# Attention and MLP decode step with gradients: query weights in pairs of groups, row vectors in fixed places, wider products, grad_out first, a new order

## The chip, the cores and the metric

The kernel runs on one core of a Trainium2 chip. The metric is device time in microseconds from start to end of one execution; the number compared is the median of several runs of the same kernel. The profile is that of one further execution, taken by the hardware profiler.

The engines named below are PE (matrix products; PEld is its loading of weights), DVE (vector), ACT (scalar), POOL (GpSimd) and SP, which here only issues transfers. Sixteen DMA engines move the data between HBM and the on-chip memory SBUF. Results of PE land in PSUM banks, and DVE or ACT must copy ("evict") them to SBUF before a transfer can store them.

## What is computed

One decode step of a layer, and all gradients of it for a given `grad_out`:

```python
def _A_ref(x, k_cache, v_cache, wq, wo):        # B=2, Sq=1, D=576, Hq=32, Hkv=16, Sk=4096, Dh=128
    q = (x @ wq).reshape(B, Sq, Hq, Dh).transpose(0, 2, 1, 3)
    k, v = jnp.repeat(k_cache, 2, axis=1), jnp.repeat(v_cache, 2, axis=1)
    scores = jnp.einsum("bhqd,bhkd->bhqk", q, k) * (Dh ** -0.5)
    p = softmax(scores)
    o = jnp.einsum("bhqk,bhkd->bhqd", p, v)
    return o.transpose(0, 2, 1, 3).reshape(B, Sq, Hq * Dh) @ wo
def _B_ref(x, w_gate, w_up, w_down):             # F=4608
    return ((x @ w_gate) * (x @ w_up)) @ w_down
xn = layernorm(A_x)
out = A_x + _A_ref(xn, A_k_cache, A_v_cache, A_wq, A_wo) + _B_ref(xn, B_w_gate, B_w_up, B_w_down)
# returned: out and the gradients of A_x, A_k_cache, A_v_cache, A_wq, A_wo, B_w_gate, B_w_up, B_w_down
```

All tensors are bfloat16. With two tokens there is little arithmetic per byte: every cache and weight is read once, and a gradient of the same size is written for each of them. Since there are only two tokens, each gradient is a sum of very few outer products.

## The kernel before

**Groups and steps.** The 16 key/value heads are worked in eight groups of two heads (four query heads each). A group and one of the two batch entries make a step; there are 16 steps. For a step the kernel loads two key tiles and two value tiles of 1 MB (`load_kv`, L1108; 8 KB per partition), transposes each on DVE (`turn`, L1175; the transposing helper is L464), forms scores and their gradients on PE (`score`, L1228, matmuls L1234), the softmax (L1283) and its gradient (L1339), contracts with the caches (`contract`, L1390, matmuls L1407), and writes the gradients of the caches as outer products (`head_outer`, L1244, matmuls L1255) against block-diagonal stationaries that POOL builds (L1222). Each such gradient tile of 1 MB takes four evictions of 128x1024 (L468 on ACT, L470 on DVE) into a staging tile, and then one store (`put`, L687, issued at L691).

**Per group.** `group_front` (L954) forms the query rows from the group's query weights and, from `grad_out`, the gradient of the attention output; `group_back` (L1020) closes a group: it adds to `acc` (L1060) and, with the transposed query weights, to `accx` (L1085), and starts the gradients of `wo` (`rows_outer`, L729) and of `wq`. Between the two calls the group's query weights stay on chip. They come in three transfers (`load_w`, L1123): two tails of 64 rows with 512 bytes each (L1132) and the main part of 512 rows with 1 KB each (L1136). They live in the ring `ww`, together with the weights `wo` and `w_down`.

**The MLP** is worked in nine slices of 512 columns (`mlp`, L838); gate and up weights come for two slices at a time (L1155, L1158), with rows of 2 KB.

**Row vectors.** A weight gradient such as that of `wq` is the outer product of the normalized input `xnr` (32-row quadrants of it) with a row vector, the tile Q for one group or D for one MLP slice. Q and D come from rings of six and five separate tiles. Gradients of several groups or slices are written together (`wide_outer`, L767): four groups, or four slices. For them `wide_unit` (L752) runs a matmul of 128 columns for every group and quadrant into one PSUM bank (L759):

```python
for j, rhs in enumerate(rhss):
    for aa in range(2):
        a = 2 * A + aa
        nc.tensor.matmul(o[:, aa, j * P:(j + 1) * P], lhsT=xnr[32 * a:32 * a + 32, dc * P:(dc + 1) * P],
                         rhs=rhs(a), start=True, stop=True)
```

The last 64 of the 576 rows go separately (`tail_outer`, L808, tiles `tl`, stores of 64 KB).

**Buffers.** One pool of 16 tiles of 8 KB per partition (`big`) serves keys and values as loaded (`kv`, at most 7), transposed tiles (`X`, at most 15), staging tiles (`st`, at most 4) and gate/up weights (`G`, at most 2).

**Order.** The kernel sets the order of all instructions on each engine while it is built. Each piece of work is a generator that yields requests: an operation on an engine with an estimated cost, a buffer (ACQ, REL), a wait for an event, a transfer (DMA). The class `Order` (L105) simulates these with a model of the transfers (`Lines`, constants `LM`, `LAG`) and, whenever an engine is free, takes the request with the lowest priority number among those that can start within a slack. The priorities are `pr(name, s)`: 28 per step, plus tables of offsets by kind and step (`PR`, `HEAD`, `TAIL`, `OFF`) and start points (`MLP_AT`, `WQ_AT`, `WO_AT`). The result is one fixed list per engine. All loads and stores but those of the inputs `A_x` and `grad_out` stand in the one list of SP, so that a store whose data aren't ready holds back the loads behind it. `A_x` and `grad_out` are issued by ACT (L597), and the layer norm waits for both.

Of the kernel before, what the change touches and what calls it, by code (L numbers as in the profile page):

```python
# [13 lines left out]
P = 128  # L14
# [90 lines left out]
class Order:  # L105
# [3 lines left out]
    def __init__(self):  # L109
        self.free = {e: 0.0 for e in ("PE", "ACT", "DVE", "POOL", "SP")}  # L110
        self.slots = {}
        self.home, self.cap, self.used = {}, {}, {}
        self.lines = Lines()
        self.quad, self.kind = (None, 0.0, 0.0), None
        self.streams = []
        self.count = 0
        self.log = []
        self.lanes = {"HW": [], "SW": []}
# [17 lines left out]
    def advance(self, s, value):  # L136
        while True:
# [13 lines left out]
            elif kind == "spawn":  # L151
                self.spawn(s.req[1], s.req[2], s.ready)
            elif kind == "prio":
                s.prio = (s.req[1], s.prio[1])
            elif kind == "lset":
                s.req[1].t = Late(s.land)
            elif kind == "lrel":
                self.pool(s.req[1])[s.req[2]] = s.land
                if s.req[1] in self.used:
                    self.used[s.req[1]] -= 1  # L160
            else:
                return

# [31 lines left out]
    def run(self):  # L195
        while self.streams:
# [8 lines left out]
            if e is not None:  # L205
                t, _, s, e = min((c for c in cand if c[3] == e and c[0] <= t + SLACK[e]), key=lambda c: (c[1], c[0]))
# [27 lines left out]
            elif r[0] == "dma":  # L234
                self.free[e] = t + r[2]
                s.land = self.lines.push(e == "POOL", t + r[2] + LATENCY[e], r[3], r[4])
# [54 lines left out]
def DMA(engine, cost, nbytes, row=8192):  # L291
# [5 lines left out]
NBIG, NGU, NWW, NBD = 16, 1, 6, 3  # L297
CAP = {"kv": 7, "X": 15, "st": 4, "G": 2}
OFF = {"mload": {0: 96.4, 1: -26.1, 2: 880.0, 3: 94.9, 4: -346.4, 5: -156.4, 6: -87.6, 7: 8.9, 8: 146.0, 9: -13.8,
       10: 91.2, 11: -99.0, 12: -61.7, 13: 103.4, 14: 404.9, 15: -150.5}, "wload": {0: -50.8, 1: -238.8, 3: -315.1,  # L300
# [7 lines left out]
       "load": {0: 195.1, 2: 227.9, 3: -17.9, 4: -185.2, 5: -111.1, 6: -195.0, 7: -157.8, 8: 475.0, 10: 90.3,  # L308
       11: -45.9, 12: -113.2, 13: 340.9, 14: 38.7, 15: -10.9}, "front": {1: -351.4, 2: 56.5, 3: 55.5, 4: 1100.6,
       5: 44.1, 6: -364.2, 7: -8.3, 8: -150.0, 10: 278.3, 11: -217.9, 12: 25.9, 14: -46.2, 15: 809.6},  # L310
       "turn0": {0: -96.0, 1: 186.1, 2: 128.2, 3: 344.6, 4: 259.4, 5: 502.5, 6: 22.0, 7: -80.7, 8: 79.6, 9: -81.7,
       10: -397.2, 11: -241.3, 12: -223.5, 13: -195.7, 14: 186.3, 15: 55.8}, "con": {0: -121.6, 1: 346.9, 2: 7.7,
# [3 lines left out]
       "back": {0: 413.0, 1: -6.1, 2: 233.5, 3: 588.7, 4: 263.1, 5: -92.6, 6: -1063.1, 7: 111.3, 8: 44.4, 10: -315.0,  # L316
# [3 lines left out]
       11: -7.4, 12: 14.8, 13: 23.1, 14: 398.8, 15: -591.6}, "dsc": {0: -130.6, 2: -312.2, 3: -339.0, 4: 207.7,  # L320
       5: -530.4, 6: 41.2, 7: 323.6, 8: -0.4, 9: 644.8, 10: -274.2, 11: 125.7, 12: 309.5, 13: -43.5, 14: 192.2,
       15: -0.7}, "mlp": {0: 81.6, 1: -71.7, 2: 147.3, 3: -224.1, 4: -6.3, 5: 14.7, 6: 616.7, 7: -152.4, 8: -159.9,
       9: 42.7, 10: -45.7, 11: 24.0, 12: 245.6, 13: -6.0, 14: -127.2, 15: -22.4}, "att": {0: 251.8, 1: -520.9,
       2: 62.8, 3: 21.5, 4: -199.3, 5: -366.7, 6: 546.7, 7: -109.6, 8: -638.2, 9: 1.5, 10: -174.3, 11: 113.2,
       12: 18.4, 13: -79.6, 14: -31.8, 15: -12.4}, "conv": {1: 208.9, 2: -233.1, 3: 119.4, 4: 0.3, 5: -102.3,
       6: -60.5, 8: 9.6, 9: -114.9, 10: 102.5, 11: 45.1, 12: 165.0, 13: -36.7, 14: 23.6, 15: -54.5}}
MLP_AT = [1.22, 5.43, 16.39, 14.23, 25.87, 33.08, 39.74, 38.29, 101.55]
WQ_AT = [-2, 5, 9, 22, 32, 30, 50, 47]
WO_AT = [-10, -14, -8, 3, 37, 36, 48, 48]
# [6 lines left out]
HEAD = {"turn0": -109.2, "turn1": -1091.6, "att": -224.6, "dsc": -208.3, "con": 390.9, "out1": -1503.4,  # L336
        "out0": 772.1, "front": 803.5, "back": -715.7, "W0": 1770.6, "W1": 26.3, "BD1": 1384.3, "BD0": 3893.2,
        "conv": -396.6, "load": 469.8}
TAIL = {"turn0": -167.6, "turn1": 1451.8, "att": -1608.9, "dsc": 1030.3, "con": 1577.7, "conv": 3.8, "out1": 2595.4,
        "out0": -474.0, "front": -576.5, "back": 355.2, "W1": 698.1, "BD1": -2114.1, "BD0": 951.5, "load": 618.9,  # L340
        "W0": 381.9}
PR = {"turn0": 410.8, "turn1": -89.2, "att": -1586.1, "dsc": -1566.9, "conv": 32.7, "con": -332.6, "out1": 2476.3,
      "out0": 866.1, "front": 94.3, "back": -196.2, "W0": -1406.3, "W1": -128.9, "BD1": 1706.7, "BD0": -477.7,
      "mlp": -490.2, "wout": -771.6, "store": -4.6, "load": 401.7, "wload": -1959.2, "fin": -1327.7, "const": 3504.2,
      "mload": -416.2}
# [8 lines left out]
def kernel(  # L354
# [45 lines left out]
    WB = 4 * FS + 256  # L400
# [10 lines left out]
    kv_t = X_t = st_t = G_t = tiles("big", NBIG, [P, NCH * Dh])  # L411
# [4 lines left out]
    tl_t = tiles("tl", 2, [P, FS])  # L416
    BD_t = tiles("BD", NBD, [P, 16, Dh])
# [3 lines left out]
    D_t = tiles("D", 5, [P, 2, P])  # L421
# [12 lines left out]
    Q_t = tiles("Q", 6, [P, P])  # L434
# [125 lines left out]
    Emore, Ein, Eprep = Event(), Event(), Event()  # L560
# [19 lines left out]
    def front_y():  # L580
        yield WAIT(Ein)
# [11 lines left out]
    def front():  # L593
        xb, yb = xy[:, 0:D], xy[:, D:2 * D]
        for t, src in ((xb, A_x), (yb, grad_out)):
            yield DMA("ACT", 0.45, 2304, 1152)
            nc.scalar.dma_start(t, src.rearrange("b s d -> (b s) d"))  # L597
        yield ("lset", Ein)
        yield SPAWN(front_y(), -999.0)
# [61 lines left out]
    def stationaries(i, rep, npos, half, costs):  # L661
# [6 lines left out]
        for h in range(2):  # L668
# [5 lines left out]
    def dxn(dp, i, X, S, pos, xoff, xstep, Xt, St, toff, tpos):  # L674
# [6 lines left out]
        for s in range(St):  # L681
            for q in range(4):
                nc.tensor.matmul(dp[32 * q:32 * q + 32, P:160], lhsT=view(Wt[:], 0, P, 8 * tpos(q, s), [[1, 32]]),
                                 rhs=view(Xt, 0, P, toff(q, s), [[2, 32]]),
# [67 lines left out]
    def wide_unit(rhss, dc, A, st, off):  # L752
        n = len(rhss)

        def mms(o):
            for j, rhs in enumerate(rhss):
                for aa in range(2):
                    a = 2 * A + aa
                    nc.tensor.matmul(o[:, aa, j * P:(j + 1) * P], lhsT=xnr[32 * a:32 * a + 32, dc * P:(dc + 1) * P],  # L759
                                     rhs=rhs(a), start=True, stop=True)  # L760
# [4 lines left out]
        return mms, (0.053 * n, 0.052 * n), 2 * P * n, ev  # L765

    def wide_outer(rhss, dst, p, event):  # L767
        width, last = FS * len(rhss), []
        for d0 in (0, 2):
            i = yield ACQ("st")  # L770
# [5 lines left out]
            for c in range(2):  # L776
                for A in range(2):
                    yield SPAWN(unit(*wide_unit(rhss, d0 + c, A, st_t[i], c * width), done[2 * c + A]), p)
# [780 lines left out]
```

## Time and profile before

| | us |
|---|---|
| median of 3 runs | 477.73 |
| lowest, highest | 476.86, 479.79 |
| the profiled execution, whole | 480.7 |
| its span, first to last instruction | 478.9 |

| engine | busy us | share of span | instructions |
|---|---|---|---|
| PE | 375.8 | 78% | 6538 |
| PEld | 214.9 | 45% | 6538 |
| DVE | 369.2 | 77% | 708 |
| ACT | 335.6 | 70% | 507 |
| POOL | 152.0 | 32% | 208 |

The granted PE clock is 0.70 on average, changing between half and full speed. In 41,925 packets 185.95 MB are moved, 388 GB/s on average: 92.48 MB read from HBM and 92.48 MB written.

The profile's page shows the span in 40 slices of 12 us; a digit is the busy share in tenths, DMA is the mean over the 16 engines. "SPq L691 <- ACT big L468" means that SP's list stood at a store (L691) until an eviction on ACT (L468) was done; the three numbers are the sum in us, the count and the longest. A transfer line ends with its size in KB and the median time from issue to landing in us. In a group's line stand the output and input tiles, the count, the busy time, the mean duration in ns and the idle time before it.

### The profile page before, as it was taken

The page shows a single profiled execution, that of the slowest core. Times are in us where ns is not written, and L with a number is a line of the kernel's source. Part 1 is how long each engine was busy: PE and PEld are TensorE (multiplying, and loading weights), DVE is VectorE, ACT ScalarE, POOL GpSimd, SP SyncE. Part 2 cuts the span into 40 slices and gives each one's busy share as a digit, 9 for nine tenths or more (in the row PEclk, how much of TensorE's full clock was granted, in tenths as well). Part 3 has the DMA queues.
Part 4 walks back from the last instruction along what each step waited for, and adds up shares of the span by engine and source line. Part 5 has one row for each costly group of instructions (what it writes and reads, how often), then busy time and mean ns, then how long its engine had stood idle before and what let it go on. Part 6 is the DMA issues. An engine that isn't in the chain of part 4 may idle for free.

```text
span 478.9 us, 15380 instructions
## 1 busy us (share of the span) xinstructions
PE 375.8 (78%) x6538; PEld 214.9 (45%) x6538; DVE 369.2 (77%) x708; ACT 335.6 (70%) x507; POOL 152.0 (32%) x208
## 2 busy tenths in 40 slices
PE   1668588989878877768878986599887769898894
PEld 1545353545554534446344453464444424444452
DVE  8788787867867976786956987889677958888781
ACT  3139659966787693833869875399776978897871
POOL 0440074343003643003434530032644556333000
PEclk9979676556766677885567595859656876656876
DMA  8999999999999999999999999999999999999994
GB/s 299 355 405 419 391 402 380 353 377 422 422 400 371 395 365 393 423 414 389 316 399 384 354 402 422 421 413 406 346 414 415 418 419 422 419 417 391 425 369 187
DMA packets 41925, 185.95 MB, mean 388 GB/s; under 512 B 3960, under 2 KB 13440, under 8 KB 25472
## 3 DMA queue, kind: packets, MB, share of 16 engines
q1 hardware_dynamic: 41848, 184.96, 98.3%
q8 instruction: 51, 0.84, 0.7%
q14 instruction: 18, 0.15, 0.1%
q10 hardware_dynamic: 8, 0.00, 0.0%
HBM read 92.48 MB, written 92.48 MB: 386 GB/s over the span
## 4 chain that ended last, share of the span: by engine, by line
DMA 46%; PE 25%; DVE 14%; ACT 8%; issue 3%; SPq 2%; POOL 1%; DVEq 0%; ACTq 0%; POOLq 0%
DMA out_dram<-big 18%; DMA big<-in_A_v_cache_dram 15%; DVE big L464 8%; ACT big L468 7%; PE ps_o L1255 4%; DMA big<-in_A_k_cache_dram 4%; PE ps_m L1234 4%; PE ps_m L1407 4%; PE ps_o L722 3%; DMA gu<-in_B_w_up_dram 3%; DMA ww<-in_A_wo_dram 3%; DMA big<-in_B_w_gate_dram 2%; DVE big L470 2%; PE ps_m L678 1%; PE ps_o L759 1%
## 5 line engine op out<-in xcount | busy, mean ns | idle before, releaser
L468 ACT CAST big<-ps_o 128x1024 bf16<-128x1024 f32 (+2 forms) x310 | 277.6, 958 | 47.6 <-PE ps_o L1255 18.9
L464 DVE STREAM_TRANSPOSE big<-big 128x1024 f32<-128x1024 f32 x146 | 175.9, 1224 | 29.7 <-DMA out_dram<-big 16.2
L1222 POOL TENSOR_TENSOR BD<-vr,mask 128x2048 bf16<-128x2048 bf16 x32 | 115.3, 3603 | 105.4 <-ACT vr L468 49.8
L470 DVE CAST big<-ps_o 128x1024 bf16<-128x1024 f32 (+2 forms) x68 | 74.2, 1093 | 16.4 <-PE ps_o L722 7.4
L1234 PE MATMUL ps_m<-big,W 128*32 128x128 bf16 x2048 | 59.9, 282 | 11.3 <-DVE cr L1359 2.6
L1234 PEld LDWEIGHTS <-W 128*32 128x32 bf16 x2048 | 46.7, 125 | 27.9 <-issue 25.7
L1255 PE MATMUL ps_o<-BD,dd 32*128 32x512 bf16 x256 | 45.8, 480 | 9.9 <-ACT big L468 7.9
L671 POOL COPY wt<-wm 64x128 bf16<-64x128 bf16 (+1 forms) x34 | 8.9, 261 | 138.2 <-DVE wm L664 119.5
L1255 PE MATMUL ps_o<-BD,pp 32*128 32x512 bf16 x256 | 48.2, 520 | 5.5 <-ACT big L468 4.0
L1199 POOL COPY W<-rep 32x16 bf16<-32x16 bf16 x128 | 24.5, 192 | 55.8 <-DVE rep L983 33.6
L464 DVE STREAM_TRANSPOSE big<-ww 128x1152 f32<-128x1152 f32 x25 | 34.0, 1359 | 7.7 <-DMA ww<-in_B_w_down_dram 3.5
L1407 PE MATMUL ps_m<-big,pp 128*32 128x512 bf16 x256 | 30.2, 547 | 3.8 <-DMA big<-in_A_v_cache_dram 3.3
L1255 PEld LDWEIGHTS <-dd 32*128 32x128 bf16 x256 | 12.2, 98 | 32.1 <-issue 27.6
L1407 PE MATMUL ps_m<-big,dd 128*32 128x512 bf16 x256 | 25.8, 491 | 0.4 <-DVE oT L1427 0.2
L1255 PEld LDWEIGHTS <-pp 32*128 32x128 bf16 x256 | 10.4, 97 | 28.1 <-issue 24.2
L872 PE MATMUL ps_m<-big,Wdy 128*128 128x128 bf16 x162 | 15.4, 269 | 4.8 <-DVE rz L1320 3.1
L722 PE MATMUL ps_o<-dyr,hb 32*32 32x288 bf16 x288 | 18.0, 382 | 0.2 <-ACT big L468 0.2
L759 PEld LDWEIGHTS <-xnr 32*128 32x128 bf16 x368 | 12.9, 116 | 10.8 <-issue 9.7
L722 PE MATMUL ps_o<-dyr,R 32*32 32x288 bf16 x256 | 16.2, 378 | 1.3 <-ACT big L468 0.9
L872 PEld LDWEIGHTS <-Wdy 128*128 128x128 bf16 x162 | 13.6, 121 | 6.8 <-issue 6.7
L759 PE MATMUL ps_o<-D,xnr 32*128 32x128 bf16 x256 | 13.0, 276 | 3.9 <-issue 2.2
L1308 ACT COPY mr<-m 1x128 f32<-1x128 f32 x16 | 4.7, 295 | 15.8 <-DVE m L1306 15.6
(205 smaller groups left out, 487.3 us busy)
## 6 DMA issues: line engine op xcount, KB each, us to landing
out_dram<-big SPq DMA_DIRECT2D x74, 1024.0 KB, 12.8
big<-in_A_k_cache_dram SPq DMA_DIRECT2D x32, 1024.0 KB, 12.7
big<-in_A_v_cache_dram SPq DMA_DIRECT2D x32, 1024.0 KB, 13.2
out_dram<-big SPq DMA_DIRECT2D x17, 576.0 KB, 10.7
ww<-in_B_w_down_dram SPq DMA_DIRECT2D x9, 576.0 KB, 13.5
ww<-in_A_wo_dram SPq DMA_DIRECT2D x8, 576.0 KB, 7.3
ww<-in_A_wq_dram SPq DMA_DIRECT2D x8, 512.0 KB, 8.0
big<-in_B_w_gate_dram SPq DMA_DIRECT2D x4, 1024.0 KB, 12.3
```

Of the source, the lines that this page charges most:

```text
L464: nc.vector.transpose(out, in_)
L468: nc.scalar.copy(out, in_)
L470: nc.vector.tensor_copy(out=out, in_=in_)
L671: nc.gpsimd.tensor_copy(view(Wt[:], 64 * h, 64, 0, [[dims[-1][1], n], [1, dims[-1][1]]]), view(Wm[:], 64 * h, 64, off, dims))
L722: nc.tensor.matmul(o[32 * q:32 * q + 32, aa, 0:HD2], lhsT=view(t, 32 * q, 32, 2 * A + aa, [[4, 32]]), rhs=dyr[32 * q:32 * q + 32, k * HD2: ...
L759: nc.tensor.matmul(o[:, aa, j * P:(j + 1) * P], lhsT=xnr[32 * a:32 * a + 32, dc * P:(dc + 1) * P], rhs=rhs(a), start=True, stop=True)
L872: nc.tensor.matmul(dh, lhsT=Wdy[:, e, 2 * k:2 * k + P], rhs=view(X[:], 0, P, 64 * k + e, [[D, FC], [2, 32]]), start=(k == 0 and e == 0), s ...
L1199: nc.gpsimd.tensor_copy(view(W_t[t][w][:], 32 * a, 32, 6 + 8 * a, [[G * WW, 4], [WW, G], [1, 2]]), view(rep_t[grp[g]["qs"]][:], 32 * a, 32 ...
L1222: nc.gpsimd.tensor_tensor(BD_t[i][:], view(vr_t[v][:], 0, P, 0, [[0, 16], [1, Dh]]), view(mask16[:], 0, P, 0, [[1, 16], [0, Dh]]), ALU.mult)
L1234: nc.tensor.matmul(sc[32 * cq:32 * cq + 32, :], lhsT=view(W[:], 0, P, (be * G + l) * WW + 6 - 4 * c2 - 2 * l, [[1, 32]]), rhs=view(X[:], 0 ...
L1255: nc.tensor.matmul(o[:, k, :], lhsT=pr2[32 * c4:32 * c4 + 32, :], rhs=BD[32 * c4:32 * c4 + 32, 8 * l + 4 * h2:8 * l + 4 * h2 + 4, :], star ...
L1407: nc.tensor.matmul(ct[32 * j:32 * j + 32, :], lhsT=view(rT, 0, P, 4 * c + 2 * l, [[1, 32]]), rhs=kv_t[kvS[s][t][l]][:, Dh * c:Dh * (c + 4) ...
```

## The change

- **Query weights.** The first two groups still come alone (1 KB rows), the other six in three pairs: one main transfer of 512 rows with 2 KB each, and two tails of 64 rows with 1 KB. They no longer live in the ring `ww` (6 tiles, now 4) but in the pool `big` (16, now 17), at most two of its tiles, and their tails in a new ring `qt` of two tiles. A pair's tile is released when the second of its groups has transposed its half. `group_front` and `group_back` read their half of the tile; in `group_back` the tail takes 16 narrow matmuls over 64 partitions in place of 8 over 128.
- **Row vectors** Q and D lie side by side in one tile each, with four fixed places (group or slice modulo four).
- **Wider products.** `wide_unit` runs one matmul over up to 512 columns for each quadrant.
- **grad_out** is loaded first on SP, ahead of the first keys; the layer norm waits for `A_x` alone.
- **Staging.** The caps of the pool change (`X` 15 to 8, `st` 4 to 9). The second tile of a head's pair, and the second half of a wide product, ask for their staging tile only after some evictions of the first.
- **Order.** All priorities, start points, slacks and the constants `LM` and `LAG` are new. The planner can now weigh loads against stores on SP (`ALT`), with a weight of 0.

```diff
-NBIG, NGU, NWW, NBD = 16, 1, 6, 3
-CAP = {"kv": 7, "X": 15, "st": 4, "G": 2}
+NBIG, NGU, NWW, NBD = 17, 1, 4, 3
+CAP = {"kv": 7, "X": 8, "st": 9, "G": 2, "wq": 2}
...
-LM, LAG = 0.67, 1.7
+LM, LAG = 0.24, 2.75
...
-BIAS = 0.196
-SLACK = {"PE": 0, "ACT": 0.21, "DVE": 0.48, "POOL": 937075237.61, "SP": 6210463039.22}
+BIAS = 0.091
+SLACK = {"PE": 0.07, "ACT": 0.32, "DVE": 0.47, "POOL": 1756923746230.71, "SP": 2641436507915.03}
...
     def front_y():
-        yield WAIT(Ein)
+        yield DMA("SP", 0.36, 2304, 1152)
+        nc.sync.dma_start(xy[:, D:2 * D], grad_out.rearrange("b s d -> (b s) d"))
+        yield ("lset", Eiy)
+        yield PRIO(-999.0)
+        yield WAIT(Eiy)
...
-    def wide_unit(rhss, dc, A, st, off):
-        n = len(rhss)
-
+    def wide_unit(rhs, n, dc, A, st, off):
         def mms(o):
-            for j, rhs in enumerate(rhss):
-                for aa in range(2):
-                    a = 2 * A + aa
-                    nc.tensor.matmul(o[:, aa, j * P:(j + 1) * P], lhsT=xnr[32 * a:32 * a + 32, dc * P:(dc + 1) * P],
-                                     rhs=rhs(a), start=True, stop=True)
+            for aa in range(2):
+                a = 2 * A + aa
+                nc.tensor.matmul(o[:, aa, 0:n * P], lhsT=xnr[32 * a:32 * a + 32, dc * P:(dc + 1) * P],
+                                 rhs=rhs(a), start=True, stop=True)
...
+    def q_rhs(g, n=1):
+        return lambda a: view(Q_all[:], 32 * a, 32, P * (g % 4), [[P, n], [1, P]])
...
+    def free_wq(pair):
+        yield WAIT(*pair["turned"])
+        yield REL("wq", pair["w"])
+        yield REL("qt", pair["t"])
...
-        yield DVE(1.37)
-        t32(pairs(X[:, 0:WB]), pairs(wq[:]))
-        yield REL("ww", st["wq"])
+        yield DVE(1.25)
+        t32(pairs(X[:, 0:4 * FS]).rearrange("p (c n) -> p c n", c=4),
+            pairs(wq[:]).rearrange("p (c n) -> p c n", c=4)[:, :, HFS * j:HFS * (j + 1)])
+        yield DVE(0.4)
+        t32(pairs(X[64 * j:64 * j + 64, 4 * FS:5 * FS]), pairs(wt[64 * j:64 * j + 64, :]))
+        yield SET(pair["turned"][j])
...
+                js = [j] if i < 2 else [0, 1] if j == 0 else []
+                for k in js:
+                    yield DMA("SP", 0.36, 64 * FS * 2, 1024)
+                    nc.sync.dma_start(t[64 * k:64 * k + 64, :], A_wq[512:576, n0 + FS * (k - j):n0 + FS * (k - j) + FS])
+                if js:
+                    yield ("lset", *[grp[i + k - j]["Lq"] for k in js])
+                    width = FS * len(js)
+                    yield DMA("SP", 0.4, 128 * 4 * width * 2, 2 * width)
+                    nc.sync.dma_start(w[:].rearrange("p (c n) -> p c n", n=2 * FS)[:, :, FS * js[0]:FS * js[0] + width],
+                                      A_wq[0:512, n0:n0 + width].rearrange("(c p) n -> p c n", p=P))
...
-    def head_outer(s, t, l, pr2, done):
+    def head_outer(s, t, l, pr2, done, after):
         g, b = divmod(s, Bq)
+        yield WAIT(*after)
         i = yield ACQ("st")
...
+    od.spawn(front_y(), -2e5)
```

More of the change, by code (lines that the diff above doesn't have):

```diff
@@ L115, in __init__ @@
         self.streams = []
+        self.last = None
         self.count = 0
@@ L155, in advance @@
             elif kind == "lset":
-                s.req[1].t = Late(s.land)
+                for e in s.req[1:]:
+                    e.t = Late(s.land)
             elif kind == "lrel":
@@ L162, in advance, with again, stores @@
                 return
+    def again(self, s, e):
+        return ALT if e == "SP" and self.stores(s) == self.last else 0.0
+    def stores(self, s):
+        return s.gen.__name__ in ("put", "final_out", "final_dx")
     def start(self, s):
@@ L205, in run @@
             if e is not None:
-                t, _, s, e = min((c for c in cand if c[3] == e and c[0] <= t + SLACK[e]), key=lambda c: (c[1], c[0]))
+                t, _, s, e = min((c for c in cand if c[3] == e and c[0] <= t + SLACK[e]),
+                                 key=lambda c: (c[1][0] + self.again(c[2], e), c[1][1], c[0]))
             r = s.req
@@ L235, in run @@
                 self.free[e] = t + r[2]
+                if e == "SP":
+                    self.last = self.stores(s)
                 s.land = self.lines.push(e == "POOL", t + r[2] + LATENCY[e], r[3], r[4])
@@ L339 @@
[L339 to L345, printed above, removed]
+ALT = 0.0
@@ L348, in pr @@
+PR = {"turn0": 544.1, "turn1": -318.2, "att": -1984.1, "dsc": -1493.2, "conv": 288.5, "con": -530.9, "out1": 1889.6,
+      "out0": 1063.4, "front": -189.5, "back": -267.9, "W0": -1094.9, "W1": 243.2, "BD1": 1052.4, "BD0": -299.5,
+      "mlp": -247.6, "wout": -893.4, "store": -2106.8, "load": 1804.4, "wload": -2440.2, "fin": -496.9,
+      "const": 3883.5, "mload": -2076.5}
 def pr(name, s):
@@ L409, in tiles @@
         return [const.tile(list(shape), dtype, name=f"{tag}{i}") for i in range(n)]
-    kv_t = X_t = st_t = G_t = tiles("big", NBIG, [P, NCH * Dh])
+    kv_t = X_t = st_t = G_t = wq_t = tiles("big", NBIG, [P, NCH * Dh])
     od.share("big", CAP)
@@ L416 @@
     tl_t = tiles("tl", 2, [P, FS])
+    qt_t = tiles("qt", 2, [P, FS])
     BD_t = tiles("BD", NBD, [P, 16, Dh])
@@ L433 @@
     R_t = tiles("R", 2, [P, P])
-    Q_t = tiles("Q", 6, [P, P])
+    Q_all = const.tile([P, 4, P], BF16, name="Qall")
+    D_all = const.tile([P, 4, 2, P], BF16, name="Dall")
+    for i in range(4):
+        od.ring(f"Q{i}", 1)
+        od.ring(f"D{i}", 1)
     pp_t = tiles("pp", 2, [P, 2, P])
@@ L593, in front @@
     def front():
[L594 to L597, printed above, removed]
+        xb = xy[:, 0:D]
+        yield DMA("ACT", 0.45, 2304, 1152)
+        nc.scalar.dma_start(xb, A_x.rearrange("b s d -> (b s) d"))
         yield ("lset", Ein)
-        yield SPAWN(front_y(), -999.0)
         yield ACT(1.5)
@@ L667, in stationaries @@
         yield POOL(costs[1])
-        for h in range(2):
+        for h in hs:
             off, dims = half(h)
@@ L1167, in load_w @@
                 yield SPAWN(mlp(k, hh, sl, Lgu, Ld, d), pr("mlp", MLP_AT[k] / 4))
+    wqs = [dict(turned=events(2)) for _ in range(NG // 2)]
     def load_ws(items):
```

154 lines of the change are left out of this document (82 added, 72 removed), and 23 rows, old and new, of the table OFF.

## The prediction

> **What bounds the kernel now.** I read the slices of the page first, then its DMA queues.
>
> ```profile
> DMA  8999999999999999999999999999999999999994
> GB/s 299 355 405 419 391 402 380 353 377 422 422 400 371 395 365 393 423 414 389 316 399 384 354 402 422 421 413 406 346 414 415 418 419 422 419 417 391 425 369 187
> ...
> q1 hardware_dynamic: 41848, 184.96, 98.3%
> ```
>
> The 16 DMA engines are busy from the first slice to the last; PE (78%), DVE (77%) and ACT (70%) are not. So the time is 184.96 MB over a rate, and the rate is not constant: 422 to 425 GB/s in the good slices, 316 to 380 in others. At 422 all the way, 184.96 MB would take 438 us, 41 us under the span. To see where these go I asked for the engines' busy time in stretches of 6 us (columns: PE, PEld, DVE, ACT, POOL busy with counts, PE clock, DMA share, GB/s):
>
> ```profile
> 0.00:6.00 6.00, 0.27 (x2) 0.20 (x2) 5.00 (x41) 1.49 (x2) 0.70 (x6) 1.00 0.65 206
> 96.00:102.00 6.00, 4.96 (x28) 1.24 (x28) 4.02 (x7) 5.72 (x10) 1.54 (x8) 0.50 1.05 334
> 222.00:228.00 6.00, 5.69 (x136) 3.50 (x129) 2.98 (x11) 3.47 (x7) 1.30 (x1) 0.69 0.89 359
> 228.00:234.00 6.00, 5.72 (x69) 1.89 (x68) 5.74 (x11) 5.57 (x8) 2.28 (x11) 0.59 0.82 284
> 258.00:264.00 6.00, 4.34 (x50) 1.69 (x48) 6.00 (x10) 5.91 (x8) 1.53 (x8) 0.94 0.85 352
> 420.00:426.00 6.00, 5.46 (x107) 3.61 (x95) 4.98 (x10) 5.72 (x9) 0.00 (x0) 0.50 1.02 422
> 468.00:474.00 6.00, 3.90 (x52) 2.19 (x42) 1.97 (x10) 1.43 (x2) 0.00 (x0) 0.78 0.77 283
> ```
>
> A full stretch reads 1.02 (packets overlap a little). Against it 222-234 lacks 2.0 us of DMA work and 258-264 1.0: the queue ran dry. At 96 it is full and slow: those are the 2 KB rows of the gate and up weights. The start and the end lack more. Then SP's own waits and the landings:
>
> ```profile
> SPq L691 <- ACT big L468: 82.6, 49, 7.7
> SPq L691 <- DVE big L470: 49.9, 17, 6.8
> SPq L1117 <- DMA out_dram<-big: 31.9, 13, 4.8
> ...
> out_dram<-big SPq DMA_DIRECT2D x74, 1024.0 KB, 12.8
> ...
> ww<-in_A_wq_dram SPq DMA_DIRECT2D x8, 512.0 KB, 8.0
> ```
>
> SP issues nearly every transfer, in one fixed order. It stands 132 us before stores whose tile isn't evicted yet (L468, L470), and everything behind such a store stands too. A store lands 12.8 us after its issue, so SP is usually far ahead; where it isn't, the engines starve. SP also waits 32 us for a store to land before a key or value load may reuse its buffer.
>
> Last I matched the trace's packet records, by size, to the issues in their order. Undisturbed packets take 27 ns (512 B), 46 (1 KB), 84 (2 KB), 178 (4.6 KB) and 309 (8 KB). The eight 1 KB loads of the query weights average 52, their 512 B tails 28; the 2 KB gate loads 87, the up loads right behind them 106. Thirteen 1 MB transfers after the first average over 340 ns instead of 309, together about 7 us over all engines. Most start within 2 us of their issue, so with nearly nothing queued. With the 3.0 us of dry queue about **10 us are starvation**; they hang on the order in which SP and the compute engines work, not on bytes.
>
> **The change, part by part.**
>
> *Query weights.* For six of eight groups, two main loads of 512 rows x 1 KB become one of 512 x 2 KB. Priced by the gate row: 2 x 512 x 52 - 512 x 87 = 8,700 ns, over 16 engines 0.54 us, three pairs 1.6. By the up row (106) three pairs cost 0.2 more. Tails: 128 packets x 28 become 64 x 47 (the 1 KB `gu` loads), 0.04 us per group, 0.3 in all. So between -1.9 and -0.1 us; which row holds depends on what is read just before, and I take the middle, **-1.0**. SP issues 13 instead of 24 transfers for them at about 0.5 us; its waits hide that. The Trainium skill, "DMA: Bandwidth & Descriptors", Specifications, holds that descriptors of 512 B and up already run at line rate; by that this term would be 0 and the sum 1.0 us later. The trace disagrees: 512 B in 27 ns is 19 bytes per ns and engine, 8 KB in 309 is 26.5.
>
> *grad_out first, on SP.* Its issue (0.24 and 0.54 us for the two issues on ACT) stands ahead of the first key load and so of the whole queue, which is full from 6 us on: **+0.4**. In exchange its two packets go ahead of the key's 1 MB. Behind it they started only at 5.09 us, while those of A_x started at 1.67, and the layer norm waited for both. Its front can run up to 3 us earlier, but the first query product needs the weights, which land at 8.6; it started at 10.6. Up to 1.9 us are gained there by compute, not by DMA, which is full of loads until the first store at 33 us. Bounds -1.9 to +0.5.
>
> *Products of 512 columns.* At L759, 368 matmuls of 128 columns become 96 of 512 or 384.
>
> ```profile
> L1255 PE MATMUL ps_o<-BD,pp 32*128 32x512 bf16 x256 | 48.2, 520 | 5.5 <-ACT big L468 4.0
> ...
> L759 PE MATMUL ps_o<-D,xnr 32*128 32x128 bf16 x256 | 13.0, 276 | 3.9 <-issue 2.2
> ```
>
> L759 holds PE for 13.0 + 6.4 us (its two groups). A 512-column matmul holds it 48.2/256 = 0.19 us, 96 of them 18: **1 to 2 us less**, and 9 us fewer weight loads beside. The evictions, which SP waits for, don't change in size. Against it, each group_back turns its query tile in 1.22 us (128x1024) plus 0.42 (the 256-column `Xt` row) instead of 1.36, DVE +2.3 us over eight groups, and has 8 more narrow matmuls (2.1 us for 64 at L683 now, so +2.1). PE comes out even. Seven of these backs lie beside other work; the eighth is on the chain that ends last (its sum into `accx` comes at 467.3, the last result's store at 473.8): **+0.3**, at most 0.6.
>
> *Buffers.* Query weights leave the `ww` ring (6 to 4) and take places in the pool (16 to 17). From load to transpose a group holds its slot now: g0 2-82, g1 24-148, g2 50-221, g3 142-254, g4 211-335, g5 235-367, g6 335-422, g7 342-467, 955 us in all, 2.0 slots on average; four remain for the rest, as before. In pairs: 2-148, 50-254, 211-367, 335-467, 638 us, 1.3 places of the pool. On average 15.7 remain against 16, but 15 while two pairs overlap. Cost on average nil.
>
> *Staging.* The cap on staging tiles goes from 4 to 9, and a head's second tile waits in the plan for two evictions of its first. Now 96 large stores pass four tiles in 479 us, so a tile has 20 us per turn. 12.8 of these are landing, so 7 remain for four to eight evictions and for SP's wait, which is up to 7.7. That is the tightest ring I find, and it stands right behind the waits at L691. I know no row for what nine buy: bounds 0 to the 10 us of starvation.
>
> *Fixed places.* D goes from five to four, Q from six to four; the next bunch's first row vector waits until the last bunch's products are done. No row shows a wait for these rings; 0, or one unit's few us if tight.
>
> The certain parts give -1.0 + 0.4 + 0.3 = **-0.3 us**. The rest is the new order. It can regain at most the 10 us of starvation and some 2 us of the end (462-474 lacks 0.8 + 1.5); it can lose more than that.
>
> **The rivals.**
>
> *Likeliest: the wider staging pays.* Half of the starvation and of the end, (10 + 2)/2 = 6 us; half because nothing in the trace puts it nearer to either bound. Sum -6.3. The profiled execution has 480.7 us (span 478.9 and 1.8 around it), 3.0 above the median of the runs: 480.7 - 6.3 - 3.0 = **471.4 us**. Its own range runs from all of it (-12 and the best rows, -1.9) to the 1% bound: 464 to 473. For it: the wait behind L691 and the four tiles. Chance 0.45.
>
> *The dry places only move.* In 66-90 and 222-234 PE is busy 4.6 to 6.0 of 6 us, partly at half clock: the evictions are late there because compute is, and no ring mends that. Then -0.3: 477.4, within 1%. Chance 0.27.
>
> *Slower: two pairs in the pool.* In 50-148, 211-254 and 335-367 one place less is left for keys, values and stores, and staging tiles may hold up to nine while they wait for landings. A place is 1 MB, 2.5 us of queue. Seven of the dry places (72, 78, 84, 140, 228, 234, 342) lie in these stretches; if each loses half to all of a place, that is 9 to 17 us, and near the lower end 477.4 + 9 = 486.4. It decides from the point where SP's wait for a landing at L1117, 4.8 us at most now, passes the 12 us or so of queue. For it: those 13 waits of 31.9 us show the pool tight already. Against it: the average of 15.7. Chance 0.28.
>
> **How the numbers follow.** The three runs lie 0.6% apart, so 1% is about what a measurement here tells from no change; the bounds are 473.0 and 482.5. The range reaches from the best case to the slower one, 464 to 487; above and below I leave out 2 in 10. Faster 0.45, within 1% 0.27, slower 0.28.
>
> **What would show it.** Right: DMA shares of 1.0 and over 400 GB/s at places like 222-264, fewer 1 MB transfers above 340 ns, shorter waits at L691. Query packets of 2 KB near 87 ns settle that term, the first key packets at 2.2 us instead of 1.8 the grad_out term. Wrong: waits at L1117 for landings well over 32 us (slower), or an unchanged sum of dry stretches elsewhere (same).

## The result, and the profile after

The changed kernel takes 495.31 us (median of 4 runs, 493.56 to 497.75) against 477.3 for the kernel before (4 runs, 476.59 to 479.79): a ratio of 1.037, 95% interval 1.031 to 1.043. It is slower, and lies above the stated range of 464 to 487 us. The span grew from 478.9 to 494.0 us, by 15.1. The granted clock is 0.69 against 0.70, and 184.96 MB are moved in both.

The page of the changed kernel, slices and transfers:

```profile
DMA  8999999999999999999999999999999999997756
GB/s 294 347 394 356 422 372 386 364 421 419 371 413 393 365 423 425 346 427 390 349 336 367 418 424 418 419 373 420 370 385 377 411 408 407 416 401 273 312 191 250
...
q1 hardware_dynamic: 39628, 184.96, 95.8%
...
out_dram<-big SPq DMA_DIRECT2D x74, 1024.0 KB, 9.9
```

The transfers' share fell from 98.3% to 95.8%, and the GB/s collapse in the last four slices: 273, 312, 191 and 250, where before has 391, 425, 369 and 187. A store now lands in 9.9 us instead of 12.8. The transfers themselves are no faster (the 8 KB packets average 323 ns, 321 before), so less stands ahead of a store in the queue. (The lines have moved: L480 transposes, L484 and L486 evict on ACT and DVE, L709 issues the stores, L1151 loads keys and values.) The same stretches as before, and then the end in stretches of 12 us (columns: PE, PEld, DVE, ACT, POOL busy with counts, PE clock, DMA share, GB/s):

```profile
222.00:228.00 6.00, 3.22 (x26) 1.94 (x26) 0.00 (x0) 1.01 (x1) 0.00 (x0) 0.50 1.01 427
228.00:234.00 6.00, 5.08 (x85) 2.49 (x83) 4.26 (x8) 4.19 (x8) 3.91 (x3) 0.78 0.90 374
258.00:264.00 6.00, 4.62 (x91) 2.63 (x89) 5.20 (x10) 5.56 (x9) 0.00 (x0) 0.78 1.02 361
420.00:426.00 6.00, 5.63 (x91) 2.77 (x88) 4.84 (x7) 5.05 (x9) 3.02 (x6) 0.50 1.00 410
```

```profile
432.00:444.00 12.00, 9.06 (x172) 4.43 (x168) 11.10 (x16) 9.50 (x13) 5.21 (x2) 0.64 1.01 404
444.00:456.00 12.00, 8.01 (x143) 4.97 (x142) 7.72 (x15) 4.46 (x10) 0.00 (x0) 0.56 0.81 299
456.00:468.00 12.00, 9.82 (x185) 5.49 (x183) 9.50 (x20) 10.24 (x15) 4.12 (x3) 1.00 0.71 290
468.00:480.00 12.00, 11.27 (x192) 6.36 (x188) 8.99 (x17) 7.81 (x12) 0.29 (x1) 0.51 0.66 223
480.00:492.00 12.00, 6.42 (x36) 2.70 (x35) 5.03 (x12) 6.04 (x7) 0.00 (x0) 0.50 0.58 241
```

The end of the kernel before, in the same columns:

```profile
444.00:456.00 12.00, 10.45 (x145) 5.22 (x141) 8.62 (x14) 10.58 (x14) 0.00 (x0) 0.85 1.02 423
456.00:468.00 12.00, 11.16 (x243) 7.70 (x241) 9.32 (x20) 9.19 (x15) 1.04 (x4) 0.72 0.95 373
468.00:478.90 10.90, 3.90 (x52) 2.19 (x42) 1.97 (x10) 1.43 (x2) 0.00 (x0) 0.66 0.44 164
```

At 222-234 and 258-264 the queue is indeed fuller than before (0.90 to 1.02 instead of 0.82 to 0.89). Most of the loss stands at the end. From 444 to 492 the DMA engines do 0.58 to 0.81 of the work they could. Comparing both traces at 450 us gives the same in bytes, by the packets that start later: 8.8 MB were left before and 10.7 MB are left after. At 425 GB/s the 1.9 MB more are 4.5 us. The remaining 10.6 us are rate: 10.7 MB took 44.0 us (242 GB/s), 8.8 MB took 28.9 (304).

What is late is compute. Of the 378 evictions into the pool's tiles 356 were done by 450 us before, 340 after. SP's list shows the same from its side, here the issue of the last value tile and the first large stores behind it, of the kernel after and then of the kernel before (start, us, what):

```profile
435.69 0.81 SPq L1151 DMA_DIRECT2D big<-in_A_v_cache_dram  x1
...
443.39 23.15 SPq L709 DMA_DIRECT2D out_dram<-big  x6
```

```profile
420.96 0.34 SPq L1117 DMA_DIRECT2D big<-in_A_v_cache_dram  x1
...
438.02 19.61 SPq L691 DMA_DIRECT2D out_dram<-big  x9
```

Six of these stores go out in 23 us, against nine in under 20, each waiting for its evictions. The last value tile is issued at 435.69, 14.7 us later than before, and the chain that ends last runs back to it; everything that follows from it, its outer products too, lies behind its landing at 445.9. POOL starts its last block-diagonal stationary at 461.22 (before at 438.19), after waiting 23.2 us for a row vector of that last step:

```profile
POOL BD L1266 <- ACT vr L484: 23.2, 1, 23.2
```

The delay gathers earlier, in stretches where the queue is full. The timeline of the kernel after around 215 us, with the PE's idle time before an instruction in brackets:

```profile
210.96 0.34 SPq L1151 DMA_DIRECT2D big<-in_A_v_cache_dram  x1
...
215.05 12.73 SPq L709 DMA_DIRECT2D out_dram<-big  x2
215.11 0.61 PE L1452 MATMUL ps_m<-big,pp 128*32 128x512 bf16 x1
...
224.78 1.04 PE L1452 MATMUL ps_m<-big,pp 128*32 128x512 bf16 x7 [9.06 <-DMA big<-in_A_v_cache_dram]
```

A value tile that PE needs at 215.7 is issued only at 210.96, after three stores, and PE goes on 13.8 us later. PE stands 9.06 us while the transfers run at 427 GB/s. A full queue thus hides the loss where it arises: it moves the transfers that are due, but not the compute that the end depends on. SP's waits, over the whole span (sum, count, longest):

```profile
SPq L709 <- DVE big L486: 103.6, 39, 11.4
SPq L709 <- ACT big L484: 99.0, 52, 9.9
SPq L1151 <- DMA out_dram<-big: 14.9, 8, 6.6
```

SP stands 203 us before stores that aren't evicted, 132 before the change. Its waits for landings at the key and value loads fell from 31.9 to 14.9. The sum of the waits before stores does not by itself tell a slow list from a fast one: of the experiments below, old_new has 127 us of them and spans 490.6, stage4 has 189 and spans 483.0.

To sum up the difference over the whole trace, I took the time of the packets that start in each stretch of 6 us as a share of 16 engines. What a stretch lacks to 1.015, about what a full one reads, I counted as dry time (the last 48 us are the last eight stretches):

| us | first 6 us | middle | last 48 us | packet time / 16 | span |
|---|---|---|---|---|---|
| before | 2.2 | 5.1 | 7.1 | 474.6 | 478.9 |
| after | 2.5 | 8.1 | 17.3 | 476.8 | 494.0 |

+0.3, +3.0, +10.2 and 2.2 us of longer packets make 15.7, against 15.1 of span.

### The profile page after: what moved, and what is told of

Read it like the earlier page. It is cut to its first block, busy times and chain, and to the rows that moved or that the text cites. A ratio compares the mean times of both kernels' runs of the same rounds, so it can differ in the third digit from the quotient of the medians.

```text
span 494.0 us, 14923 instructions
## 1 busy us (share of the span) xinstructions
PE 387.0 (78%) x6330; PEld 217.0 (44%) x6330; DVE 380.4 (77%) x718; ACT 329.5 (67%) x505; POOL 150.4 (30%) x200
## 3 DMA queue, kind: packets, MB, share of 16 engines
q1 hardware_dynamic: 39628, 184.96, 95.8%
## 4 chain that ended last, share of the span: by engine, by line
DMA 36%; PE 33%; DVE 13%; ACT 11%; issue 4%; SPq 2%; POOL 0%; DVEq 0%; ACTq 0%
DMA big<-in_A_v_cache_dram 17%; DMA out_dram<-big 12%; ACT big L484 10%; PE ps_o L1300 7%; DVE big L480 6%; PE ps_m L1452 5%; PE ps_m L1278 5%; DMA gu<-in_B_w_up_dram 4%; PE ps_o L740 3%; DVE big L486 3%; DMA big<-in_B_w_gate_dram 2%; PE ps_m L1022 2%; SPq L1200 1%; PE ps_m L696 1%; PE ps_m L892 1%
## 5 line engine op out<-in xcount | busy, mean ns | idle before, releaser
L484 ACT CAST big<-ps_o 128x1024 bf16<-128x1024 f32 (+2 forms) x296 | 265.9, 958 | 52.9 <-PE ps_o L1300 35.3
L480 DVE STREAM_TRANSPOSE big<-big 128x1024 f32<-128x1024 f32 x154 | 185.9, 1224 | 22.5 <-DMA out_dram<-big 9.7
L486 DVE CAST big<-ps_o 128x1024 bf16<-128x1024 f32 (+1 forms) x82 | 89.8, 1096 | 19.3 <-PE ps_o L740 9.2
L1278 PEld LDWEIGHTS <-W 128*32 128x32 bf16 x2048 | 48.1, 127 | 23.0 <-issue 21.8
L689 POOL COPY wt<-wm 64x128 bf16<-64x128 bf16 x26 | 7.4, 286 | 113.5 <-DVE wm L682 113.0
L1452 PE MATMUL ps_m<-big,pp 128*32 128x512 bf16 x256 | 29.2, 542 | 12.3 <-DMA big<-in_A_v_cache_dram 9.1
L1452 PE MATMUL ps_m<-big,dd 128*32 128x512 bf16 x256 | 29.9, 557 | 2.3 <-DVE dd L480 0.9
L480 DVE STREAM_TRANSPOSE big<-ww 128x1152 f32<-128x1152 f32 x17 | 23.2, 1364 | 5.9 <-DMA out_dram<-big 4.0
L1022 PE MATMUL ps_m<-big,Wdy 128*128 128x128 bf16 x144 | 15.5, 291 | 3.2 <-DVE big L480 3.2
L696 PE MATMUL ps_m<-big,wm 128*32 128x128 bf16 x416 | 13.0, 283 | 6.2 <-DVE Dall L899 4.6
L892 PE MATMUL ps_m<-big,Wdy 128*128 128x128 bf16 x162 | 16.4, 280 | 1.6 <-DVE rz L1365 1.2
L484 ACT CAST osb<-ps_m 128x512 bf16<-128x512 f32 x15 | 8.9, 592 | 13.0 <-PE ps_m L1452 13.0
L892 PEld LDWEIGHTS <-Wdy 128*128 128x128 bf16 x162 | 14.9, 128 | 4.1 <-issue 4.0
## 6 DMA issues: line engine op xcount, KB each, us to landing
ww<-in_A_wo_dram SPq DMA_DIRECT2D x8, 576.0 KB, 14.2
```

What stands on the lines that cost most here:

```text
L480: nc.vector.transpose(out, in_)
L484: nc.scalar.copy(out, in_)
L486: nc.vector.tensor_copy(out=out, in_=in_)
L696: nc.tensor.matmul(dp[32 * q:32 * q + 32, 0:P], lhsT=view(Wm[:], 0, P, 8 * pos(q, s), [[1, 32]]), rhs=view(X, 0, P, xoff(q, s), [[xstep, 4 ...
L892: nc.tensor.matmul(dh, lhsT=Wdy[:, e, 2 * k:2 * k + P], rhs=view(X[:], 0, P, 64 * k + e, [[D, FC], [2, 32]]), start=(k == 0 and e == 0), s ...
L1022: nc.tensor.matmul(dp, lhsT=Wdy[:, e, 2 * k:2 * k + P], rhs=view(X[:], 0, P, 64 * k + e, [[D, GH], [2, 32]]), start=(k == 0 and e == 0), s ...
```

## The experiments

Two theories: **order**, the new list of instructions itself costs the time, whatever the code's parts bring; and **parts**, one of the edits (transfers of 2 KB rows, the pool, the matmuls, grad_out) does. Every kernel here computes the whole reference. The kernel's own plan (the simulation by which it orders its instructions, run while it is built) gives a time at which it expects the last instruction to end. I note that as "plan": a number of the program, not of the chip. With the order the list also fixes which engine takes an eviction (310 on ACT and 68 on DVE before, 296 and 82 after) and which tile of the pool a piece of work gets; "order" means all of this.

**undo3, and each part alone.** The list of every engine is left as the change has it; three parts are put back, first together.

```diff
-        nc.sync.dma_start(xy[:, D:2 * D], grad_out.rearrange("b s d -> (b s) d"))
...
+        nc.scalar.dma_start(xy[:, D:2 * D], grad_out.rearrange("b s d -> (b s) d"))
...
-                nc.tensor.matmul(o[:, aa, 0:n * P], lhsT=xnr[32 * a:32 * a + 32, dc * P:(dc + 1) * P],
-                                 rhs=rhs(a), start=True, stop=True)
+                for j in range(n):
+                    nc.tensor.matmul(o[:, aa, j * P:(j + 1) * P], lhsT=xnr[32 * a:32 * a + 32, dc * P:(dc + 1) * P],
+                                     rhs=rhs(a, j), start=True, stop=True)
...
-                    nc.sync.dma_start(w[:].rearrange("p (c n) -> p c n", n=2 * FS)[:, :, FS * js[0]:FS * js[0] + width],
-                                      A_wq[0:512, n0:n0 + width].rearrange("(c p) n -> p c n", p=P))
+                    for k in js:
+                        nc.sync.dma_start(w[:].rearrange("p (c n) -> p c n", n=2 * FS)[:, :, FS * k:FS * k + FS],
+                                          A_wq[0:512, n0 + FS * (k - j):n0 + FS * (k - j) + FS].rearrange("(c p) n -> p c n", p=P))
```

> The changed kernel with its instruction lists untouched except for three parts, each put back in place: the pairs' query weights come in two transfers of 1 KB rows, the wide products run as matmuls of 128 columns, and grad_out is issued on ACT behind A_x. Theory 'order' (the new lists by themselves cost the time): the three parts together are worth at most 2 us either way, so 493 to 498 us and a span near 494. Rival 'parts' (2 KB rows, 512-column products or the late first key cost it): at least half of the 18 us comes back, 486 us or less.

Measured: 499.53 us, 1.0435 of before (1.0403 to 1.0466); span 498.4. Putting the parts back regains nothing; it is, if anything, 3 us slower, above the 493 to 498 that the order theory gave. So the slowdown isn't theirs. (The pool, the ring `ww` of four tiles, the fixed places and the tails stay as changed here; they are tested by the new_found runs below.) To see whether two of them cancel, each was put back alone (`rows1k` the third hunk, `narrow` the second, `gradact` the first), beside the changed kernel again:

> The changed kernel as it is, beside the next three on one chip. Every theory: 494 to 497 us, a ratio of 1.031 to 1.043.

> The changed kernel with the same lists, but each pair's query weights in two transfers of 1 KB rows, one behind the other. With all three parts undone the kernel took about 3 us longer than the changed one. If the rows carry that: +2 to +4 us against the changed kernel. By the packets, 2 x 512 x 51 ns against 512 x 98 ns over 16 engines, three pairs: +0.4 us.

> The changed kernel with the same lists, but the wide products run as matmuls of 128 columns: 272 matmuls more. If PE's length carries the 3 us: +2 to +4 us against the changed kernel. If it lies beside the transfers: within 1 us.

> The changed kernel with the same lists, but grad_out issued on ACT behind A_x. The prediction's term says -0.4 us (the first key load goes out earlier). If the earlier start of the front carries the 3 us: +2 to +4 us against the changed kernel.

| | median us | ratio to before | 95% interval | span |
|---|---|---|---|---|
| changed_again | 495.54 | 1.0382 | 1.0356 to 1.0408 | 492.9 |
| rows1k | 496.19 | 1.0388 | 1.0364 to 1.0413 | 492.8 |
| narrow | 495.33 | 1.0371 | 1.0353 to 1.0389 | 493.2 |
| gradact | 495.46 | 1.0372 | 1.0345 to 1.0399 | 489.5 |

None of them differs from changed_again by more than 0.13%, well inside the intervals. A part alone is worth nothing that can be measured under this list. Why the three together seem to cost 3 us stays open; the intervals of undo3 and changed_again touch. (The span is that of the one profiled execution, and gradact's was its fastest.)

**The order carried across.** `new_old` is the code of the change with all numbers of before (priorities, start points, caps, 17 places in the pool); `old_new` the code before with all numbers of the change. The main lines of new_old's edit, whose tables of priorities are left out here:

```diff
-CAP = {"kv": 7, "X": 8, "st": 9, "G": 2, "wq": 2}
+CAP = {"kv": 7, "X": 15, "st": 4, "G": 2, "wq": 2}
...
-LM, LAG = 0.24, 2.75
+LM, LAG = 0.67, 1.7
```

> The changed kernel's code with all numbers of the kernel before (priorities, start points, slacks, caps, LM and LAG), and 17 pool tiles and 4 ww tiles as changed. Its plan ends at 471.8. Theory 'order': numbers found for one code don't fit another; span about 494 (471.8 + 22.5), 491 to 498 us. Rival 'numbers' (only the new tables are bad, the code is as good as before): 475 to 481 us. Rival 'code' (buffers and waits of the new code cost the 18 us whatever the numbers): also about 495, so this run speaks against 'numbers' alone and needs the next one.

> The code of the kernel before with all numbers of the changed one, and 16 pool tiles and 6 ww tiles as before. Its plan ends at 473.6. Theory 'order': span about 496 (473.6 + 22.5), 493 to 500 us. Rival 'code' (the new code's buffers and waits cost it): the old code stays near 477 to 482 us. Rival 'numbers': about 495.

Measured: new_old 492.99 us, 1.0329 (1.0268 to 1.0390); old_new 491.77, 1.0273 (1.0243 to 1.0304). Both crosses are slow: neither code is good with the other's numbers. old_new came out a little below the 493 to 500 us expected. This doesn't tell order from parts yet, since numbers for another code are no fair list for it. It does show that numbers which are good for one program aren't good for another that does nearly the same work.

**stage4.** The change with the pool's caps of before, all else untouched:

```diff
-CAP = {"kv": 7, "X": 8, "st": 9, "G": 2, "wq": 2}
+CAP = {"kv": 7, "X": 15, "st": 4, "G": 2, "wq": 2}
```

> The changed kernel with one line different: the caps of the pool are again 15 for X and 4 for staging; the lists follow from that anew. The kernel's own plan of its work ends at 456.4 us for the kernel before, 471.5 for the changed one and 464.8 for this one. Theory 'order': the chip follows the plan, whose ends differ by as much (15.1) as the spans (494.0 and 478.9); so a span of about 487 (464.8 + 22.5) and 486 to 490 us. Rival 'pool' (staging tiles crowd out the loads): the whole loss goes with the cap, 480 us or less. Third: the cap is beside the point, 493 to 497.

Measured: 484.8 us, 1.0131 (1.0099 to 1.0163); span 483.0. This is just below the range of the order theory and well above that of the pool rival. Four staging tiles instead of nine give back 11 of the 15 us of span. That looks like the pool's crowding, but the plan contradicts it. Under this list a cap of 6, 7, 8, 9, 10 or 11 gives one and the same plan of 471.5; five tiles give 468.2, four 464.8, three 475.7; the cap on `X` between 6 and 15 does nothing. Nine are thus never reached: in the plan not more than six staging tiles are out at once. Lowering the cap shifts the list, and that is what counts. The end of stage4, in the same columns as above:

```profile
456.00:468.00 12.00, 10.61 (x204) 5.93 (x205) 9.41 (x20) 11.23 (x19) 0.87 (x3) 0.87 0.86 320
468.00:480.00 12.00, 10.29 (x154) 6.34 (x152) 6.60 (x17) 8.07 (x10) 0.00 (x0) 0.64 0.79 308
```

It is dry for 6.5 us in the last 48 instead of 17.3, while its waits for landings (15.6 us at L1151) are as in the change: the wait that crowding would raise didn't move. Its last value tile is issued at 433.29, nearly as late as in the change, so a late last tile alone does not carry the 15 us.

**old_one.** If the order alone can cost this much, it should do so in the kernel before too, with no part of the change at all. One priority of one step is moved, one whose move makes the plan end 14.6 us later:

```diff
-       5: -530.4, 6: 41.2, 7: 323.6, 8: -0.4, 9: 644.8, 10: -274.2, 11: 125.7, 12: 309.5, 13: -43.5, 14: 192.2,
+       5: -530.4, 6: 41.2, 7: 323.6, 8: 59.6, 9: 644.8, 10: -274.2, 11: 125.7, 12: 309.5, 13: -43.5, 14: 192.2,
```

> The kernel before with one of its numbers changed: the offset of 'dsc' at step 8 from -0.4 to 59.6. Nothing of the change is in it. Plan 471.0 us instead of 456.4. Theory 'order': the same loss as the whole change, span 488 to 494, 487 to 496 us. Rival (the plan of old code is no guide, the loss belongs to the new code): 476 to 481 us.

Measured: 495.05 us, 1.0329 (1.0301 to 1.0356); plan 471.0, span 492.1. The same code, work and bytes, and nearly the whole slowdown. Its end:

```profile
468.00:480.00 12.00, 11.95 (x194) 7.36 (x193) 7.14 (x16) 8.03 (x12) 0.47 (x2) 0.50 0.71 274
480.00:492.00 12.00, 4.90 (x26) 2.06 (x24) 2.86 (x11) 4.72 (x6) 0.00 (x0) 0.50 0.55 219
```

Here 12.3 us of dry time lie in the middle and 10.9 in the last 48.

**new_found, new_found2, new_found3.** The other direction: the code of the change, not one operation altered, with numbers searched anew, each step kept if the plan ends earlier. The first and the third end at 452.1 and 451.9 in the plan, the second, from the numbers of before, at 455.3. The lists of new_found and new_found3 differ on every engine. The caps of the three are 5, 3 and 17 staging tiles.

```diff
-CAP = {"kv": 7, "X": 8, "st": 9, "G": 2, "wq": 2}
+CAP = {'G': 2, 'X': 18, 'kv': 7, 'st': 5, 'wq': 2}
```

> The changed kernel's code, all parts in, LM and LAG as changed, with priorities, start points, caps (staging 5, X 18), BIAS and slacks searched again from the changed ones by 8,236 random steps that kept an earlier end of the kernel's own plan. Plan 452.1 us (changed 471.5, before 456.4). Theory 'order': the chip follows: span 469 to 475 (the distances to the plan seen so far are 17.0 to 22.5), 468 to 476 us, at or a little below the kernel before. Rival 'code' (buffers, pairs in the pool and fixed places cost it on the chip): 484 us or more in spite of the plan.

> The same code, searched from the numbers of the kernel before (LM 0.67, LAG 1.7, staging 3, X 25) by 8,488 steps. Plan 455.3 us. Theory 'order': 472 to 480 us. Rival 'code': 484 us or more. If this and the last differ by much more than their plans (3.2 us), the model's LM and LAG matter on the chip.

> The code of the change with a third list of instruction order, found by another search of its numbers; the kernel's own plan ends at 451.9 us (the list of new_found: 452.1), with places for 17 staging tiles and 8 of the value pairs allowed, and a different order on every engine. Theory, the order that was found sets the time and the plan's end says how much: the span is 473 to 478 us, the time 474 to 481 us, 0.99 to 1.01 of before. Rival, a wide staging cap crowds the pool: the span is 484 us or more. The distance between this run and new_found also tells how much two lists of equal plan differ on the chip.

Measured: new_found 479.77 us, 1.0015 (0.9995 to 1.0034); new_found2 482.98, 1.0080 (1.0058 to 1.0103); new_found3 480.71, 1.0066 (1.0038 to 1.0094). The slowdown is gone to within 0.8% while every part of the change stands. The first two missed the ranges that the order theory gave (468 to 476 and 472 to 480): a plan up to 4.3 us earlier than that of before brought no gain on the chip. The end of new_found, and SP's waits before its stores (L1011 is the store there, L786 and L788 the evictions on ACT and DVE):

```profile
432.00:444.00 12.00, 10.00 (x123) 4.56 (x119) 10.04 (x17) 9.81 (x15) 3.60 (x1) 0.62 0.80 281
444.00:456.00 12.00, 10.70 (x214) 6.38 (x209) 10.64 (x23) 10.56 (x14) 0.58 (x2) 0.93 1.01 422
456.00:468.00 12.00, 11.29 (x184) 7.17 (x183) 10.29 (x19) 7.86 (x13) 0.29 (x1) 0.60 0.95 357
468.00:480.00 12.00, 2.55 (x14) 1.33 (x14) 1.09 (x5) 1.31 (x2) 0.00 (x0) 0.56 0.35 142
```

```profile
SPq L1011 <- ACT big L786: 74.1, 45, 5.3
SPq L1011 <- DVE big L788: 51.6, 21, 10.9
```

After a dry stretch at 432 it is full to 456, and it has 126 us of waits before stores, near the 132 of the kernel before. new_found3, with 17 staging tiles allowed, of which its plan uses six at once as the change's does, waits 64 us for landings (32.4 at the key and value loads, 31.5 at the stores) and is still within 0.7% of before: a wide cap and long waits for landings don't make a kernel slow by themselves. But two lists whose plans are 0.2 us apart differ by 0.5% on the chip, and span minus plan goes from 17 to 27 us below, so the plan ranks lists only to within several us.

All of them, with the plan beside the chip:

| | code | plan | span | span - plan | ratio |
|---|---|---|---|---|---|
| before | before | 456.4 | 478.9 | 22.5 | 1 |
| old_one | before | 471.0 | 492.1 | 21.1 | 1.0329 |
| old_new | before | 473.6 | 490.6 | 17.0 | 1.0273 |
| after | change | 471.5 | 494.0 | 22.5 | 1.0371 |
| undo3 | change, parts back | 471.5 | 498.4 | 26.9 | 1.0435 |
| stage4 | change | 464.8 | 483.0 | 18.2 | 1.0131 |
| new_old | change | 471.8 | 491.3 | 19.5 | 1.0329 |
| new_found | change | 452.1 | 477.3 | 25.2 | 1.0015 |
| new_found2 | change | 455.3 | 481.2 | 25.9 | 1.0080 |
| new_found3 | change | 451.9 | 476.1 | 24.2 | 1.0066 |

The four lists that plan 452 to 456 lie at 476 to 481 on the chip, the four that plan 471 to 474 (undo3 aside) at 491 to 494, whichever code. The change's plan is 15.1 us later than before's, as is its span; with distances between plan and span of 17 to 27 us, that these agree to a tenth is chance.

How far each set of numbers is from a minimum of its own plan can be seen by moving every priority, offset and start point, one at a time, up and down by 100 (moves with which no list comes about are left out):

```
numbers of    plan    moves    plan unchanged    earlier by over 0.1 us    best gain
before       456.4     670          586                   3                 0.25
after        471.5     666          605                  41                11.0
```

No single move of this size gains the numbers of before more than 0.25 us; they stand near the bottom of their valley. Those of the change don't stand at the bottom of any, for the code they came with, and a search from them got to 452.1. Most moves leave the plan's end where it is, so old_one shows how much one number can cost, not what one usually costs. None of the three searched lists beats the kernel before on the chip.

## Why the prediction was wrong

**The step that failed** is the term for the new order: "half of the starvation and of the end, (10 + 2)/2 = 6 us", credited to the wider staging. It came out as +15 us. I bounded what an order can regain from dry places of the trace, noted that it can lose more, and put no price on that side. The runs supply it: with one number changed the order costs 3.3%, and the lists here whose plans end late cost 4 to 15 us of span, which dwarfs every other term. The new order did fill the places named in the forecast, 222-234 and 258-264, but it emptied others (240-252 reads 0.94 instead of 1.03): the dry time of the middle grew from 5.1 to 8.1 us, that of the end from 7.1 to 17.3. The forecast's other signs went the wrong way too: 17 instead of 13 transfers of 1 MB average over 340 ns, and the waits before stores rose from 132 to 203 us.

**The staging cap** of nine gave nothing. The plan never uses more than six, and with four the change was 10 us faster. "A tile has 20 us per turn" was true, but a tight ring in an order that fits it isn't a bottleneck: new_found2 plans with three staging tiles and spans 481.2.

**Query weights**, forecast -1.0 us. By the packets: before, eight groups of 512 x 52 ns and 1,024 x 28 ns over 16 engines, 15.1 us; after, two of 512 x 49, three pairs of 512 x 98 and 512 x 53, 14.2 us: -0.9, right. The 2 KB rows took 98 ns here and 92 to 96 in the other lists of this code, between the gate and up rows that bounded them. The Trainium skill, "DMA: Bandwidth & Descriptors", Specifications, by which rows of 512 B already run at line rate, would have given 0; the packets disagree with it by this 0.9 us, and the whole time (rows1k) can't tell the two apart.

**grad_out**, forecast +0.4 against a faster front: the first key packets start at 2.1 us instead of 1.8, and the first product of the front at 3.06 instead of 5.73, the first product of the normalized input at 6.86 instead of 8.62, the first query product at 9.64 instead of 10.60. Mechanism as told, worth nothing that gradact could measure: what the front gained was not what the end waited for.

**Products of 512 columns**, forecast 1 to 2 us less on PE and 9 us fewer weight loads: 18.5 instead of 19.4 us, a little under the range, and 4.7 instead of 12.9 of loads. The larger of its groups:

```profile
L774 PE MATMUL ps_o<-Dall,xnr 32*128 32x512 bf16 x64 | 12.9, 517 | 2.1 <-ACT big L484 1.6
```

0.20 us each, as the row of the outer products (0.19) had said. In group_back the eight short transposes take 3.4 us, as forecast (0.42 each). The narrow matmuls were mis-sized: 128 of them take 2.3 us where 64 took 2.1, so they add 0.2 us and not 2.1, and PE comes out 0.7 us ahead on both counts instead of even. The narrow run shows that the length of the products does not reach the end.

**The rivals.** "Slower: two pairs in the pool" had the right sign and the wrong mechanism. It named its own test, waits for landings at the key and value loads well over 32 us, and they fell to 14.9. Its 486.4 was 9 us short. "The dry places only move" described the middle and gave no room for the end. The range reached to 487 because the only price on the slow side was a place in the pool.

**What stays open**: why the numbers that came with the change weren't at a minimum for its code, whether another list would let the change's parts win their 1 us, and the 3 us of undo3. Which single decision in the list costs most wasn't tried on the chip: the late value tile at 211 and the last one at 436 are read from the trace, not isolated, and stage4 with its last tile at 433 speaks against the latter as the only cause.

## What to carry to other kernels

When a change brings a newly found order, split it in two before judging: the parts under an unchanged order, and the order under unchanged parts. Treat the order as a term with a loss as large as anything it was meant to gain, and test whether its numbers are at a minimum for the exact program by moving some of them one at a time. Where an in-order list issues all transfers, read the end first: a queue that is full in the middle can hide that compute falls behind, and the bill comes in the last slices.

## What the runs showed that I had not expected

Packet time over 16 engines is nearly the same in all these kernels, 470 to 479 us, while their spans go from 476 to 498: transfers got little slower, most of the difference is dry time of the DMA engines (15 us in new_found3, 28 in the change). Stores landed faster in the slow kernel (9.9 us against 12.8), so a shorter landing need not be a good sign; it is no sure sign of a slow list either, since old_new is slow with 13.6 us. And 272 more matmuls with 272 more weight loads (narrow) changed nothing that can be measured (1.0371 against 1.0382) on an engine that is busy 78% of the span.
